# One fp32 attention and MLP kernel on one core: a new order of all its steps, without the warm-up steps behind the first, and with three instead of one joined product in seven sweeps

## The chip, the core and the metric

The kernel runs on one core of one Trainium2 chip. The time is that of one execution on the device, in microseconds (us); the timed runs of a kernel are told by their median. Of the engines TensorE (PE) does matmuls into PSUM (eight banks of 512 fp32 columns), VectorE (DVE) and ScalarE (ACT) read PSUM and SBUF, and SyncE (SP) issues nearly all transfers, in one queue and in order. GpSimd has almost nothing to do.

## What is computed

```python
def attention(x, state):            # x: 8 x 8 x 512 x 64, state: 8 x 8 x 32 x 64
    a = softmax(x @ state.T / 8)    # every row of x reads the 32 rows of state
    xread = a @ state
    a2 = softmax(state @ x.T / 8)   # every row of state reads the 512 rows of x
    sread = a2 @ x
    return concatenate([xread, sread], axis=2)     # 544 rows of 64 per head

x = attention(...).transpose(0, 2, 1, 3).reshape(4352, 512)
h = x @ w_in                        # 512 x 2048
g = log(1 + exp(h))                 # softplus
out = g @ w_out                     # 2048 x 512
```

All in fp32, with outputs of 8 x 544 = 4352 rows of 512.

## The kernel before

An fp32 number is held as a high and a low part, and one fp32 product is three matmuls in a faster format: high by high, high by low, low by high. A split into the two parts is one ACT copy (names that end in `h`: `gh`, `vh`, `wh`) and one DVE subtraction behind it (`gl`, `vl`, `wl`; line 328).

The weights come as 64-bit words and are turned into fp32 by three steps each: `ch` on ACT, `cu` and `cr` on DVE. The letter behind a step's name in the table of steps chooses the form: `ch` is an activation Prelu (letter A, which needs its own table load on ACT) or a Copy (C, which needs none); `cu` is one int32 operation (V) or two uint16 operations (W).

For each of the 8 batches b: the scores (`B.Qb`, from `Lz.b` and `Lt.b.i`, loads of state and x), a softmax over state in steps `qk`, `A`, `M`, `Ms`, `m` (Exp), `N`, `Nm`, `D`, `ah`, `al`; the first product of the MLP with state folded into w_in (`B.Vb.c`), `h.b.f` (six matmuls of 512 columns into one bank, 16 values of f), softplus `s`. The softmax the other way is `E` (row maximum), `e` (Exp), `r`, `H` (a transpose on DVE, stored by `Se` and loaded again by four `Le.b.j`), then the read group `B.Rb` (64 matmuls), `X.b` (a scaling), `T.b`, `th`, `tl`. The rows of state of all batches are a ninth batch, `h.8`, at the end.

The second product of batch 0 is done directly (steps `m.0.f.c`, accumulated in four banks). That of the other batches is done in 15 sweeps (b, s), each over half of a batch's rows, by a scheme with 7 products for 8 (Strassen's, in Winograd's form). A sweep has 8 blocks u; a block needs the stored softplus values (`Tr`, a load from `td`), three DVE additions `sfa`, `sfb`, `sfc` (lines 744 to 747), a split `gh`, `gl` of 128x896, and then on PE the steps `p.b.s.u.j`: X and Y with two products each, Z with two, Q with one. The sums of products stay in banks over the 8 blocks and are then added together by `e1` to `e6` (`e1` on ACT, the others on DVE at line 773; Z by one 128x512 operation `e5`).

A product with 256 columns is three matmuls of 256 columns (line 766). Product 6 (Q) is *wide* in all sweeps but the last: high by high and high by low are one matmul of 512 columns (line 762), low by high one of 256 (line 763) into the same bank, whose two halves are added when it is emptied. So a wide product takes a whole bank:

```python
if pi in wide:
    nc.tensor.matmul(at(bank), g(0), r(wform(u, m)(slice(0, 2))), start=first, ...)
    nc.tensor.matmul(at(bank)[:, 0:256], g(1), r(wform(u, m)(0)), start=False, ...)
    continue
```

The order of everything is a table, `PLAN`, written out by hand: 2833 entries `step:engine:places`, where T is PE, A and C are ACT, V and W are DVE, S is the SP queue, and the places are PSUM banks (0 to 7) and slots of one SBUF arena. Each engine does its steps in the order of the table and waits where data or a place isn't ready. Steps `w.i` (line 615) are warm-up steps: two transposes of the identity into a bank that nobody reads. The table names 14 of them; ten matmuls at the program's start (line 888) are apart from these.

Of the kernel before, what the change touches and what calls it, by code (L numbers as in the profile page):

```python
# [960 lines left out]
```

## Time and profile before

| | before |
|---|---|
| time, three runs | 630.94 us median (630.7 to 631.95) |
| profiled execution | 633.1 us, of which the span of instructions is 631.3 |
| PE busy | 617.0 us, 98% |
| DVE busy | 504.0 us, 80% |
| ACT busy | 397.2 us, 63% |
| granted TensorE clock | 1.00 throughout |
| HBM | 222 GB/s |

The span runs from the first to the last instruction of the profiled execution. PE's matmuls overlap at their ends, so that a busy share near 100% says that it rarely waited and not that each matmul is as short as it could be. Table loads aren't counted as busy time of ACT.

### The profile page before, as it was taken

The numbers are of one execution on the slowest core, as the hardware profiler recorded it, in microseconds if no ns is written. First come the engines' busy times: TensorE is split into PE (matmuls) and PEld (weight loads), VectorE is DVE, ScalarE is ACT, GpSimd is POOL, SyncE is SP. The second block draws the span as 40 slices with busy tenths as digits, with TensorE's granted clock in tenths as the row PEclk, the third lists the DMA queues.
The fourth block names the chain that finished last, engine by engine and source line by source line (L and its number), as shares of the span: only waits on it lengthen the run. The fifth ranks groups of instructions, "written<-read, shape, count | busy, mean of one in ns | idle before, by whom it ended". The sixth has DMA issues, their size and how long they took to land.

```text
span 631.3 us, 12414 instructions
## 1 busy us (share of the span) xinstructions
PE 617.0 (98%) x4604; PEld 530.2 (84%) x4604; DVE 504.0 (80%) x1081; ACT 397.2 (63%) x659; POOL 1.0 (0%) x7
## 2 busy tenths in 40 slices
...
GB/s 343 415 226 327 289 232 240 255 231 399 353 19 216 193 200 254 294 206 281 241 294 319 255 189 257 266 224 124 288 128 271 208 246 141 138 107 33 152 51 35
DMA packets 64253, 141.07 MB, mean 223 GB/s; under 512 B 7360, under 2 KB 17600, under 8 KB 64192
## 3 DMA queue, kind: packets, MB, share of 16 engines
...
HBM read 83.10 MB, written 57.15 MB: 222 GB/s over the span
## 4 chain that ended last, share of the span: by engine, by line
PE 70%; DVE 14%; DMA 10%; issue 2%; ACT 2%; SPq 2%; DVEq 0%; ACTq 0%
PE h L331 21%; PE pk_X L766 9%; PE pk_Y L766 9%; PE pk_Z L766 9%; PE acc L331 7%; DVE arena L328 4%; DMA arena<-td 3%; PE pk_Q L762 3%; PE h L820 2%; PE vp L331 2%; DMA arena<-vd 2%; PE vq L331 2%; SPq L319 1%; DVE arena L744 1%; PE pk_Q L763 1%
## 5 line engine op out<-in xcount | busy, mean ns | idle before, releaser
L312 ACT CAST arena<-arena 128x512 fp32r<-128x512 f32 (+2 forms) x255 | 185.8, 763 | 140.2 <-DVE arena L747 46.5
L328 DVE TENSOR_TENSOR arena<-arena,arena 128x512 fp32r<-128x512 f32 (+2 forms) x255 | 213.5, 858 | 58.3 <-ACT arena L312 56.1
L331 PE MATMUL h<-arena,arena 128*128 128x512 f32 x760 | 190.3, 399 | 0.0
L331 PEld LDWEIGHTS h<-arena,arena 128*128 128x128 f32 x760 | 138.3, 188 | 40.0 <-issue 4.2
L766 PE MATMUL pk_Y<-arena,arena 128*128 128x256 f32 x720 | 106.2, 284 | 0.4 <-DVE arena L328 0.4
L766 PE MATMUL pk_X<-arena,arena 128*128 128x256 f32 x720 | 105.5, 283 | 0.0
L766 PE MATMUL pk_Z<-arena,arena 128*128 128x256 f32 x696 | 103.8, 284 | 0.4 <-DVE arena L328 0.4
L766 PEld LDWEIGHTS pk_X<-arena,arena 128*128 128x128 f32 x720 | 96.6, 189 | 5.9
L766 PEld LDWEIGHTS pk_Y<-arena,arena 128*128 128x128 f32 x720 | 94.9, 190 | 1.1 <-DVE arena L328 0.6
L766 PEld LDWEIGHTS pk_Z<-arena,arena 128*128 128x128 f32 x696 | 92.2, 191 | 1.8 <-issue 0.8
L719 ACT ACTIVATE arena<-h 128x512 f32<-128x512 f32 x112 | 66.6, 613 | 29.8 <-PE h L331 25.7
L744 DVE TENSOR_TENSOR arena<-arena 128x256 f32<-128x256 f32 x120 | 49.5, 419 | 25.0 <-DMA arena<-td 23.9
L331 PE MATMUL acc<-arena,arena 128*128 128x512 f32 x192 | 45.7, 396 | 0.0
L762 PE MATMUL pk_Q<-arena,arena 128*128 128x512 f32 x112 | 44.8, 401 | 0.0
L331 PEld LDWEIGHTS acc<-arena,arena 128*128 128x128 f32 x192 | 35.8, 188 | 8.1 <-issue 1.0
L747 DVE TENSOR_TENSOR arena<-arena 128x128 f32<-128x128 f32 x120 | 33.6, 287 | 1.7
L746 DVE TENSOR_TENSOR arena<-arena 128x128 f32<-128x128 f32 x120 | 33.4, 287 | 1.4
L763 PE MATMUL pk_Q<-arena,arena 128*128 128x256 f32 x112 | 31.4, 280 | 0.0
L820 PE MATMUL h<-sreadT,arena 128*128 128x512 f32 x64 | 22.8, 393 | 0.0
L762 PEld LDWEIGHTS pk_Q<-arena,arena 128*128 128x128 f32 x112 | 21.3, 190 | 1.3 <-issue 0.8
L378 DVE SCALAR_TENSOR_TENSOR arena<-arena,arena 128x512 int32<-128x512 int32 x31 | 21.0, 688 | 0.5
L763 PEld LDWEIGHTS pk_Q<-arena,arena 128*128 128x128 f32 x112 | 21.3, 190 | 0.0
...
## 6 DMA issues: line engine op xcount, KB each, us to landing
...
arena<-td SPq DMA_DIRECT2D x112, 256.0 KB, 4.4
...
```

The source lines that it names most:

```text
L312: nc.scalar.copy(dst, src)
L328: lambda e: eng(e).tensor_tensor(r(dlo()), src(), dhi(), ALU.subtract))
L331: nc.tensor.matmul(dst, lhs, rhs, start=start, stop=stop)
L378: nc.vector.scalar_tensor_tensor(u, h2().bitcast(I32), 3, u, ALU.logical_shift_left, ALU.bitwise_or)
L719: nc.scalar.activation(t[:, :, 0::3] if i == 0 else t[:, :, 1:3], src.rearrange("p (s c t) -> p s c t", s=2, t=P), AF.Softplus)
L744: op(f"sfa.{k}", "V", t, [f"t.{k}:a"], lambda e, g=blocks: nc.vector.tensor_tensor(g()[:, 0:2], g()[:, 4:7:2], g()[:, 7:8].broadcast_to([P ...
L746: op(f"sfb.{k}", "V", [t[0], f"t.{k}:a"], [f"t.{k}:b"], lambda e, g=blocks: nc.vector.tensor_tensor(g()[:, 2], g()[:, 1], g()[:, 4], ALU.add))
L747: op(f"sfc.{k}", "V", [t[1], f"t.{k}:b"], [f"t.{k}:c"], lambda e, g=blocks: nc.vector.tensor_tensor(g()[:, 3], g()[:, 5], g()[:, 2], ALU.s ...
L762: nc.tensor.matmul(at(bank), g(0), r(wform(u, m)(slice(0, 2))), start=first, stop=False, skip_group_check=True)
L763: nc.tensor.matmul(at(bank)[:, 0:256], g(1), r(wform(u, m)(0)), start=False, stop=True, skip_group_check=True)
L766: nc.tensor.matmul(at(bank)[:, 256 * half:256 * half + 256], g(gi), r(wform(u, m)(wi)), start=first and pi == ps[0] and i == 0, stop=i == ...
L820: nc.tensor.matmul(hb, r(w[:, 0, cs]), r(at("sreadT")[:, :, kt, :]), start=kt == 0, stop=False, skip_group_check=True)
```

## The change

`PLAN` is a new table with 2897 entries. `WIDE` names seven sweeps in which products 4, 5 and 6 are wide: Z's two products then take a bank each (Z and W) and a step each, so that a block has five steps of PE (`p.b.s.u.2` is Z, `.3` W, `.4` Q) and a sweep five banks, and `e5` becomes four additions of 128x256 (`e5`, `e5l`, `e7`, `e7l`). The code for that was there and not in use. Of the warm-up steps only `w.0` stays. The forms of some steps change: `cu.2.0` to `cu.2.3` from W to V and `ch.2.0` to `ch.2.3` from C to A, `cu.o3` from V to W and `ch.o3` from A to C, with three such pairs later; `X.1` and `X.7` go from ACT to DVE. Of the table the diff shows the line with most of the warm-up steps, and the line of the new table with the step that follows them.

```diff
-WIDE = {}
+WIDE = {(4, 1): (4, 5, 6), (5, 0): (4, 5, 6), (5, 1): (4, 5, 6), (6, 0): (4, 5, 6), (6, 1): (4, 5, 6), (7, 0): (4, 5, 6), (8, 0): (4, 5, 6)}
...
-ah.1.0:A:42 Wl.0:V: ah.0.0:A:32 w.4:T:2 w.5:T:2 w.6:T:2 w.7:T:2 w.8:T:2 w.9:T:2 w.10:T:2 w.11:T:2 m.0.3.3:T: Wl.1:V: ah.0.1:A:34 al.1.0:V: D.1.1:T:2 Lo.4:S:38
...
+Li.2.0:S:22 D.1.0:T:1 wl.3:V: m.0.2.2:T: ah.1.0:A:24 N.1.1:V: m.0.3.3:T: Lo.4:S:26 Nm.1.1:V: cu.1.0:V:28 D.1.1:T:4 cu.1.1:V: m.0.3.1:T: al.1.0:V: ah.1.1:A:42
...
-            used = [f"acc.{b}.{x}.{c}:{f1}" for b, x, f0, fe in RUNS if f0 <= f1 < fe for c in range(4)]
+            used = [f"W.{f1}:u{b}{c}" for b in PLAIN for c in range(4)]
...
-            op(f"m.{k}.{c}", "T", [f"g.{k}:h", f"g.{k}:l", f"W.{f}:h", f"W.{f}:l"] + ([f"{acc}:{f - 1}"] if f > f0 else []), [f"{acc}:{f}"], gemm2)
+            op(f"m.{k}.{c}", "T", [f"g.{k}:h", f"g.{k}:l", f"W.{f}:h", f"W.{f}:l"] + ([f"{acc}:{f - 1}"] if f > f0 else []), [f"{acc}:{f}", f"W.{f}:u{b}{c}"], gemm2)
```

The last two edits name differently what `Wh` waits for, with the same effect. All lines behind the table are five further down in the changed kernel.

Three places of the new order follow, each before and after. First DVE near the end of the ramp, before: from the last softmax product of batch 1 (`Nm.1.1`, L464) to the low part `al.1.0` of its transposed softmax (the last row). Between them are `cfa`, `cfb` (L595, L597: combinations of w_out) and five splits (L328), the third of them `gl.0.3`.

```order
L464 TENSOR_TENSOR arena_432<-arena_432,sm 128x512
L595 SCALAR_TENSOR_TENSOR arena_185<-arena_314,arena_317 128x256
L595 SCALAR_TENSOR_TENSOR arena_185<-arena_416,arena_314 128x256
L597 TENSOR_TENSOR arena_317<-arena_317 128x256
L597 TENSOR_TENSOR arena_314<-arena_314 128x256
L328 TENSOR_TENSOR arena_414<-vp_0_1_366,arena_414 128x512
L328 TENSOR_TENSOR arena_499<-arena_416,arena_499 128x512
L328 TENSOR_TENSOR arena_502<-arena_183,arena_502 128x512
L328 TENSOR_TENSOR arena_384<-arena_317,arena_384 128x256
L328 TENSOR_TENSOR arena_425<-arena_314,arena_425 128x256
L328 TENSOR_TENSOR arena_508<-ab_0_486,arena_508 128x512
```

The same place on DVE in the changed kernel: from the splits `gl.0.3` and `wl.3` (the first two rows) over the second softmax sum and product (L463 to L469) to `al.1.0`.

```order
L333 TENSOR_TENSOR arena_454<-arena_425,arena_454 128x512
L333 TENSOR_TENSOR arena_459<-arena_403,arena_459 128x512
L463 TENSOR_REDUCE sm<-arena_403 128x16
L464 TENSOR_SCALAR sm<-sm 128x16
L465 RECIPROCAL sm<-sm 128x16
L469 TENSOR_TENSOR arena_403<-arena_403,sm 128x512
L375 TENSOR_SCALAR arena_190<-arena_246 128x512
L375 TENSOR_SCALAR arena_190<-arena_257 128x512
L333 TENSOR_TENSOR arena_487<-ab_0_478,arena_487 128x512
```

The combinations and the two half splits of 128x256 are gone from here; the splits stand ahead of the softmax product, and behind it come only two `cu.1.q` (L375).

Second the SP queue around the loads for `B.Q6`, before: `in_zp_dram` is `Lz.6` (state), `in_xt_dram` are `Lt.6.0` and `Lt.6.1` (x), `td` and `te` are spilled values.

```order
L319 DMA arena_2338<-in_xt_dram 128x1024
L322 DMA out_dram<-arena_185 128x512
L319 DMA arena_2510<-td_110 128x512
L319 DMA arena_767<-td_111 128x512
L319 DMA arena_185<-in_xt_dram 128x1024
L322 DMA td_126<-arena_2988 128x1024
L319 DMA arena_3438<-td_113 128x512
L319 DMA arena_2673<-in_zp_dram 128x256
```

And in the changed kernel, from `Lz.6` to `Lt.6.1`:

```order
L324 DMA arena_403<-in_zp_dram 128x256
L327 DMA out_dram<-arena_2216 128x512
L324 DMA arena_2885<-td_112 128x512
L324 DMA arena_2086<-td_110 128x512
L327 DMA te_71<-arena_337 128x512
L327 DMA te_71<-arena_3216 128x512
L324 DMA arena_403<-qd_81 128x512
L324 DMA arena_2216<-td_111 128x512
L324 DMA arena_3410<-in_xt_dram 128x1024
L327 DMA td_126<-arena_2897 128x1024
L324 DMA arena_337<-in_xt_dram 128x1024
```

The state load stood behind both x loads and now stands ahead of both.

Third DVE in sweep (3,0), before: the rows up to the split `gl.3.0.7` (the last row) and behind `gl.3.0.5`; L438 is the transpose `A.6.g` of the scores of batch 6.

```order
L746 TENSOR_TENSOR arena_3438<-arena_3438 128x128
L747 TENSOR_TENSOR arena_3438<-arena_3438 128x128
L744 TENSOR_TENSOR arena_949<-arena_949 128x256
L746 TENSOR_TENSOR arena_949<-arena_949 128x128
L438 STREAM_TRANSPOSE arena_2673<-sc_1_3678 128x512
L438 STREAM_TRANSPOSE arena_2347<-sc_0_3677 128x512
L747 TENSOR_TENSOR arena_949<-arena_949 128x128
L328 TENSOR_TENSOR arena_2044<-arena_3438,arena_2044 128x896
```

And in the changed kernel, the last twelve rows up to `gl.3.0.7`; ahead of them, behind `gl.3.0.5`, stand one more `sfa` (L749) and the two `A.6.g` (L443). L485 and L486 are `E.3.0`, L445 `M.6.g`, L459 `Ms.6.0`, L528 `H.3.0`.

```order
L751 TENSOR_TENSOR arena_2885<-arena_2885 128x128
L485 TENSOR_REDUCE nm<-arena_3202 128x1
L486 TENSOR_SCALAR nm<-nm 128x1
L752 TENSOR_TENSOR arena_2885<-arena_2885 128x128
L749 TENSOR_TENSOR arena_3685<-arena_3685 128x256
L445 TENSOR_REDUCE mx<-arena_2216 128x16
L751 TENSOR_TENSOR arena_3685<-arena_3685 128x128
L445 TENSOR_REDUCE mx<-arena_403 128x16
L752 TENSOR_TENSOR arena_3685<-arena_3685 128x128
L459 TENSOR_TENSOR arena_403<-arena_403,mx 128x512
L528 STREAM_TRANSPOSE arena_2216<-arena_3202 128x4x4x32
L333 TENSOR_TENSOR arena_2169<-arena_2885,arena_2169 128x896
```

Row maximum, maxima, difference and transpose have moved ahead of the split, and with them the additions of the next sweep's first block.

## Rows read from the trace of the kernel before

**Rows 1.** The page: busy time, share of span and instructions of each engine.

```profile
PE 617.0 (98%) x4604; PEld 530.2 (84%) x4604; DVE 504.0 (80%) x1081; ACT 397.2 (63%) x659; POOL 1.0 (0%) x7
```

**Rows 2.** Stretches: from:to, length, busy PE, PEld, DVE, ACT, POOL; clock, DMA share, GB/s.

```profile
44.00:60.00 16.00, 15.94 (x119) 10.33 (x118) 15.38 (x33) 15.53 (x29) 0.00 (x0) 1.00 0.82 309
100.00:160.00 60.00, 60.00 (x371) 42.21 (x370) 46.54 (x90) 58.42 (x109) 0.00 (x0) 1.00 0.76 287
250.00:270.00 20.00, 18.25 (x234) 16.46 (x233) 17.73 (x43) 12.47 (x20) 0.00 (x0) 1.00 0.93 289
290.00:310.00 20.00, 18.99 (x181) 17.08 (x181) 12.66 (x34) 11.98 (x20) 0.00 (x0) 1.00 0.75 238
330.00:350.00 20.00, 17.94 (x185) 15.34 (x184) 18.21 (x41) 14.14 (x22) 0.00 (x0) 1.00 0.93 318
350.00:370.00 20.00, 19.36 (x184) 16.98 (x183) 18.89 (x48) 14.77 (x27) 0.00 (x0) 1.00 0.78 235
550.00:600.00 50.00, 50.00 (x376) 47.93 (x375) 41.77 (x95) 25.53 (x49) 0.00 (x0) 1.00 0.31 101
```

**Rows 3.** Timeline of the ramp, all engines: start, length (us), engine, line, operation.

```profile
30.02 1.28 ACT L363 ACT_TABLE_LOAD   x1
35.25 1.28 ACT L646 ACT_TABLE_LOAD   x1
37.21 3.85 PE L615 MATMUL wp<-ident 128*128 128x128 f32 x16
38.16 1.96 DVE L328 TENSOR_TENSOR arena<-arena,arena 128x512 fp32r<-128x512 f32 x4
40.82 0.94 PE L331 MATMUL acc<-arena,arena 128*128 128x512 f32 x3
44.12 4.25 PE L331 MATMUL h<-arena,arena 128*128 128x512 f32 x18
```

**Rows 4.** DVE by line and shape: count, then busy us, mean ns, idle time.

```profile
L328 DVE TENSOR_TENSOR arena<-arena,arena 128x896 fp32r<-128x896 f32 x120 | 129.6, 1087 | 39.4 <-ACT arena L312 37.4 <-PE tp L539 1.1 <-PE pk_Q L762 0.5
L328 DVE TENSOR_TENSOR arena<-arena,arena 128x512 fp32r<-128x512 f32 x119 | 79.2, 686 | 19.0 <-ACT arena L312 18.6
L744 DVE TENSOR_TENSOR arena<-arena 128x256 f32<-128x256 f32 x120 | 49.5, 419 | 25.0 <-DMA arena<-td 23.9 <-DMA arena<-vd 0.5
L747 DVE TENSOR_TENSOR arena<-arena 128x128 f32<-128x128 f32 x120 | 33.6, 287 | 1.7
L373 DVE TENSOR_SCALAR arena<-arena 128x512 uint16<-128x512 uint16 x19 | 8.8, 462 | 0.0
L370 DVE TENSOR_SCALAR arena<-arena 128x512 int32<-128x512 int32 x13 | 5.3, 416 | 0.0
L773 DVE TENSOR_TENSOR arena<-pk_Z,arena 128x512 f32<-128x512 f32 x14 | 9.6, 682 | 0.0
L773 DVE TENSOR_TENSOR arena<-pk_Q,arena 128x256 f32<-128x256 f32 x29 | 12.1, 417 | 0.0
```

**Rows 5.** Timeline of PE at the read group `B.R4`.

```profile
250.99 0.88 PE L766 MATMUL pk_Y<-arena,arena 128*128 128x256 f32 x6
253.41 1.10 PE L331 MATMUL rp<-arena,arena 128*32 128x64 f32 x64 [1.54 <-DMA td<-arena]
```

**Rows 6.** Timeline of PE at the score group `B.Q6`.

```profile
328.71 1.56 PE L331 MATMUL h<-arena,arena 128*128 128x512 f32 x6
332.33 1.09 PE L331 MATMUL sc<-arena,arena 64*32 64x512 f32 x16 [2.06 <-DMA arena<-in_zp_dram]
```

**Rows 7.** Timeline of PE: X steps one block apart, sweeps (7,0) and (7,1).

```profile
558.13 0.87 PE L766 MATMUL pk_X<-arena,arena 128*128 128x256 f32 x6
560.63 0.88 PE L766 MATMUL pk_X<-arena,arena 128*128 128x256 f32 x6
606.65 0.88 PE L766 MATMUL pk_X<-arena,arena 128*128 128x256 f32 x6
609.17 0.88 PE L766 MATMUL pk_X<-arena,arena 128*128 128x256 f32 x6
```

More of the change, by code (lines that the diff above doesn't have):

```diff
@@ L93 @@
-B.K3.1:T:5,4 s.3.4.0:A: gl.0.7:V: ch.o10:C:64 Sv.3.2.1:S: h.2.12:T:7 cv.3.1.0:A:11 cu.o10:W:52 Td.3.4:S: cv.3.1.1:A:53 ch.o8:C:78 cr.o10:V: Sv.3.1.0:S:
-h.2.13:T:1 s.3.5.1:A: D.4.0:V:79 ch.o9:C:64 cu.o8:W:3 h.2.14:T:6 Lo.11:S:34 gh.0.8:A:88 cu.o9:W:71 gh.0.10:A:40 Lo.13:S:80 s.2.6.0:A:54 cr.o8:V: h.2.15:T:3
-Sv.3.1.1:S: wh.10:A:86 gl.0.8:V: wh.8:A:38 cr.o9:V: h.3.12:T:2 s.2.6.1:A: gl.0.10:V: Td.3.5:S: wh.9:A:16 wl.10:V: s.2.7.0:A:32 h.3.13:T:5 Td.2.6:S: wl.8:V:
-ch.o7:C:59 wl.9:V: s.2.7.1:A: cu.o7:W:78 Lo.12:S:44 h.3.14:T:4 s.3.6.0:A:96 s.3.6.1:A: cfa.4:V:64 Lv.4.0.0:S:94 cr.o7:V: m.4.1:A: h.3.15:T:0 cfb.4:V:
@@ new lines @@
+Li.3.2:S:56 vh.1.1.0:A:38 Li.3.3:S:46 vh.1.1.1:A:66 vl.1.1.0:V: Lo.5:S:76 vh.0.1.0:A:82 Lo.6:S:88 vl.1.1.1:V: h.1.3:T:0 vh.0.1.1:A:48 vl.0.1.0:V: ch.2.0:A:62
+vl.0.1.1:V: ch.2.1:A:65 h.1.5:T:6 E.0.1:V: ch.2.2:A:52 ch.2.3:A:53 cu.2.0:V:96 h.1.4:T:5 cu.2.1:V: uh.0.2:A:54 cr.2.0:V: s.1.0.0:A:58 cr.2.1:V: h.1.6:T:1
+cu.2.2:V:92 Sf.2.0:S: cu.2.3:V: cr.2.2:V: s.1.2.1:A:80 h.1.7:T:4 cr.2.3:V: s.1.2.0:A: ul.0.2:V: Sf.2.1:S: s.1.3.0:A:86 cfa.0:V:62 Lt.2.0:S:22 kh:A:18
+B.V0.2+V1.2:T:2,6,5,1 cfb.0:V: Lt.2.1:S:70 s.1.3.1:A: kl:V: Lt.3.0:S:72 ch.3.0:C:65 cfc.0:V: Lt.3.1:S:52 ch.3.1:C:94 cfd.0:V: Td.1.2:S: cu.3.0:W:38 ch.3.2:C:66
@@ new lines @@
+Sv.0.1.1:S: D.2.0:V:70 s.0.12:A:71 h.0.14:T:1 Td.1.7:S: D.2.1:V:72 ah.2.0:A:24 M.3.1:V: ah.2.1:A:42 h.0.15:T:3 Lt.4.0:S:62 al.2.0:V: s.0.13:A:73 Lt.4.1:S:80
+s.0.14:A:8 al.2.1:V: uh.2.1:A:58 Ms.3.0:V: B.K0.0:T:5,7 s.0.15:A:70 ul.2.1:V: m.3.0:A: B.V2.0+V3.0:T:4,6,2,0 Ms.3.1:V: cfa.1:V:72 cfb.1:V: cfc.1:V:
+cv.0.0.0:A:56 B.K0.3:T:1,3 Lz.4:S:57 N.3.0:V: vh.2.0.1:A:22 Sv.0.0.0:S: vh.2.0.0:A:44 vl.2.0.1:V: vh.3.0.0:A:20 vl.2.0.0:V: vh.3.0.1:A:30 B.K0.2:T:5,6
+cv.0.0.1:A:36 vl.3.0.0:V: h.2.0:T:4 cv.0.3.0:A:37 Sv.0.0.1:S: vl.3.0.1:V: cv.0.3.1:A:56 Sv.0.3.0:S: Nm.3.0:V: m.3.1:A: Sv.0.3.1:S: h.2.1:T:7 cfd.1:V:
```

427 lines of the change are left out of this document (214 added, 213 removed).

## Prediction

> **What bounds the kernel now.** I read the page first, then the busy time by stretch, then the timelines where TensorE (PE) is idle. PE works 617.0 of 631.3 us, VectorE (DVE) 504.0, ScalarE (ACT) 397.2 [rows 1], so PE bounds the whole and the span can fall in three ways only: fewer steps on PE, shorter ones, or less waiting in front of them. The stretches differ. From 44 to 60 us DVE is busy 15.38 and ACT 15.53 of 16 us [rows 2]: there PE takes what these two deliver, and the eight warm-up steps in a row at 37.21 (3.85 us, sixteen transposes) stand where PE would otherwise idle [rows 3]. From 100 to 160 us ACT is busy 58.42 of 60 and PE never stops [rows 2]. In four 20 us stretches between 250 and 370 us PE is idle 1.75, 1.01, 2.06 and 0.64 us [rows 2]: mostly loads that come late. From 550 to 600 us PE has no idle time at all [rows 2].
>
> The profiled execution took 633.1 us, 2.2 more than the median of the three timed ones (630.94). The changes below are summed against 633.1 and then set off from the median. Times of PE steps are differences of starts, since one matmul's end overlaps the next one's start.
>
> **The ramp: warm-ups out, work reordered.** Thirteen warm-up steps of two transposes go; their starts are about 0.48 us apart (3.85 us for eight), 6.3 us in all. That is not the gain, since DVE and ACT would be waited for instead. The ramp ends with `B.V0.3+V1.3`, the last group of batches 0 and 1. What stands ahead of it on DVE: out go `cfa.1` and `cfb.1` (0.42 each, priced as other 128x256 adds), `Wl.0` and `Wl.1` (the same size, 0.42 each) and `ul.0.1` (0.69); in come `Tl.0` (0.69) and `cfd.0` (0.42). Net 2.37 - 1.11 = 1.26 us less. The four `cu.2.q` turn from two uint16 operations (0.462 each; the second of the pair is of the same form and size) into one int32 operation (0.416): 0.51 less each, 2.03 in all. `cu.o3` turns the other way, 0.51 more. Net: 2.8 us less DVE work ahead of that group [rows 4]. On ACT the Exp `e.0.1`, which needs a table load before it and one behind it, now comes after the group: at 1.28 a load [rows 3] that is 2.6 us less ahead of it, beside the step itself. So DVE allows 2.8 and ACT about as much, of a possible 6.3 on PE. The first places agree. The step behind the eight warm-ups, `m.0.3.3` at 40.82, needed `gl.0.3`, the second of four operations at 38.16 (done about 39.5), and that needed `s.0.3`, which stood on ACT behind a table load at 30.02, `ch.o3`, two Exp, four `ch.1.q` and a table load at 35.25 [rows 3]. Now `ch.o3` is a Copy and `s.0.3` comes right behind it, ahead of all of these: some 5 us sooner, so that `m.0.3.3` can follow `D.1.0` at once, near 37. The next steps wait for `al.1.0` and `al.1.1`. Nine operations of 0.42 to 0.69 us stood between the last softmax product and `al.1.0`; two `cu` and the split itself stand there now (first two order excerpts). I therefore let the first `h.1.0` move from 44.12 to about 41.5. DVE and ACT stay full up to 60 us, so nothing more is gained there; from 60 to 100 us they have room. From 100 to 160 us ACT is full, with the same steps and table loads in it, so it starts sooner and ends sooner; a few tenths go where ACT's copies and softplus steps stand in a new order. **Ramp: -2.7 us**, bounds -4.2 (DVE's idle time is used as well) and -1.0 (the first steps' input loads hold it).
>
> **The middle, 230 to 430 us.** Here PE waited for loads. `B.R4` came 253.41 - 250.99 - 0.72 = 1.70 us later than the Y step before it lets it [rows 5], `B.Q6` 332.33 - 328.71 - 1.40 = 2.22 us late (1.40 is an `h` step of six matmuls at 0.23) [rows 6], `B.R1` at 291 about 1.0 (the idle time of 290 to 310) and `B.R0` at 266 some 0.2 (1.75 idle between 250 and 270, less the 1.54 of `B.R4`). Sum 5.1. Some ten further steps, each less than 0.8 us behind what steps of its kind take, come to 2.8 together (the 0.64 us between 350 and 370 are of these); 7.9 in all.
>
> What the new order does to each: `B.Q6` waited for the state load `Lz.6`, which was issued behind two `xt` loads and four `td` transfers. Now that load stands ahead of these (third and fourth excerpts), and 14 us of PE steps lie between it and the group instead of 5: the 2.22 go. `B.R4` stands one product step (0.72) later: 1.70 - 0.72 = 1.0 remains. `B.R0` and `B.R1` come 0.35 and 1.7 us of PE steps later relative to their loads: both waits go. Against this `B.R5` has 4.9 us between the last load and itself where it had 6.4, and `B.R6` 6.7 where it had 11.8. The groups that waited, above, got their data only after 6 to 7 us; so `B.R5` may wait between 0 and 2.2, for which I take 0.6. Loads after: 1.6 of the 5.1.
>
> The price is on DVE. Between `gl.3.0.5` and `gl.3.0.7`, the splits that two blocks of products wait for, stand thirteen other operations and the split itself (last two excerpts): two stacked transposes, two maxima, a difference, the row maximum and a transpose of 128x512 (seven, priced like the split of this size at 0.69; the row maximum's small scaling is left out), two triples of 0.42 + 0.29 + 0.29 and the split at 1.09 [rows 4], 8.0 us by durations and some 7 by starts (the four operations at 38.16, 2.2 us by durations, took 1.96 [rows 3]). PE has two blocks of 2.50 us to do meanwhile [rows 7]. So `p.3.0.7.1` waits about 2.0 us. Before, two of these seven stood there and the other five behind `gl.3.0.7`, where they cost PE some 1.4 of the 2.8 us in small pieces up to 365 us. A second place, the splits of sweep (2,0), and `X.5`, a scaling that the next `h` step waits for, cost perhaps 0.5 each. Small waits of 1.3 us I leave as they are. So 2.8 becomes 2.0 + 1.0 + 1.3 = 4.3. **Middle: (1.6 + 4.3) - 7.9 = -2.0 us**, bounds -4.5 (DVE's new place is covered) and +1.5 (`B.R5` waits 2.2 and the DVE places add 1.5).
>
> **The wide products.** A block of seven products with Q alone wide takes 560.63 - 558.13 = 2.50 us; in the last sweep, where Q is narrow, 609.17 - 606.65 = 2.52 [rows 7]. One wide product thus saves about 0.016 us by the blocks; by the steps themselves (0.36 for three matmuls of 256 columns, 0.35 for one of 512 and one of 256) 0.009. Seven sweeps x 8 blocks x 2 products = 112: 1.0 to 1.8 us, and I take 1.2. On DVE one 128x512 eviction (0.682) becomes four of 128x256 (0.417): 0.99 us more in each of seven sweeps [rows 4]. From 550 to 600 us DVE is busy 41.77 of 50 [rows 2], so this has cover; banks are tighter (five of eight in a sweep), for which I add 0.2. **Wide: -1.0 us**, bounds -1.8 and +0.5.
>
> On this term the Trainium skill bears (page "TensorE: Matmul & The Clock Gate", section "Back-to-back issue gap"): it gives the warm spacing of single matmuls as N/2.4 ns plus about 2.5, so that joining two of 256 columns saves one 2.5 ns. By that 112 joins would give an estimate of 0.3 us; the blocks in the trace show three to six times as much.
>
> **Sum.** -2.7 - 2.0 - 1.0 = -5.7: 627.4 on the profiled execution's time, **625.2 us** against the median. A difference under 0.2% (1.26 us) is about what a measurement of this kernel can't tell from no change.
>
> **Rivals.**
> *Waits change places.* DVE is the second engine everywhere, and the new order puts more in front of it. If `B.R5` waits in full, the DVE places cost 1.5 more than I say and ACT between 100 and 160 us gives back 1.5 of the ramp, the middle ends near +1 and the ramp at -1.2: 630.94 - 1.2 + 1 - 1 = 629.7, faster or the same. For it: 15.38 of 16 and 58.42 of 60 us busy [rows 2]. Against it: the largest single wait of before (2.2) is plainly gone. 0.18.
> *All stalls go.* The ramp gives 4.2, the middle 4.5, the wide products 1.6: 620.6. Against it: DVE's 7 to 8 us in front of a 5 us stretch. 0.10.
> *Slower: the bank squeeze.* A wide sweep holds five banks, and at its end W is free only after the evictions of X, Y and twice 0.42, each of which can stand behind a split of 1.09 [rows 4]; the next sweep's fifth bank, or an `h` group, then waits. It decides when each of the seven sweep ends costs PE more than (5.7 + 1.3) / 7 = 1.0 us; at 2 us each the time is 639. For it: DVE at 84% from 550. Against it: sweeps with four banks show no wait there at all. 0.06.
> *Slower: the clock.* The warm-ups kept PE active where it would idle. The granted clock was 1.00 (2.4 GHz) in every stretch of [rows 2], also around idle times of 1.54 and 2.06 us [rows 5, 6]. If PE now fell to 1.2 GHz from 44 to 60 us, its 15.94 us of work there would take twice as long: 630.94 - 5.7 + 15.9 = 641. The new idle pieces in the ramp are under 2 us each by my walk, so 0.02.
> The same page of the Trainium skill, in its table under "Why this matters for your kernels", warns that a PE left idle between bursts goes back to the lower clock. No run here shows that so far.
>
> **Numbers.** Forecast 0.64 (622 to 628), waits change places 0.18 (half faster, half the same), all stalls go 0.10, slower 0.08. Faster 0.83, same 0.09, slower 0.08. The range, 620.5 to 630.0, leaves out the slower cases, half of the one in which all stalls go, and the upper edge of the one in which waits change places; the forecast's own is 622 to 628.
>
> **What would show it.** Ramp: first `h.1.0` at 41 to 42, no wait over 1 us before 60; DVE or ACT still over 15 of 16 us there. Middle: no idle time at `B.Q6` and `B.R1`, about 1 at `B.R4`, some 2 us of PE waits for DVE's split in the last blocks of sweep (3,0). Wide: blocks of 2.47 to 2.49 us and no idle time on PE from 430 on. It is wrong if `h.1.0` stays near 44, if the read groups 5 or 6 wait over 2 us, or if PE waits at the ends of wide sweeps.

## The result and the profile after

The changed kernel takes 624.4 us (median of four runs, 623.81 to 624.99) against 630.82 for the kernel before in the same comparison (628.75 to 631.95): a ratio of 0.9903, 95% interval 0.9884 to 0.9922. Run once more beside other kernels it took 624.76 against 631.62, ratio 0.9894 [0.9864, 0.9925]. Forecast were 625.2 us, 620.5 to 630.0, and faster with 0.83. Its profiled execution took 624.3 us, with a span of 622.5.

The page of the changed kernel, busy time by engine and the granted clock of PE in forty slices:

```profile
PE 610.8 (98%) x4466; PEld 521.6 (84%) x4466; DVE 508.5 (82%) x1104; ACT 395.9 (64%) x655; POOL 1.0 (0%) x7
...
PEclk9999999999999999999998999999999999999999
```

PE has 6.2 us less work than in [rows 1], with 138 matmuls fewer: 112 joined ones and 26 transposes of the thirteen warm-ups. DVE has 4.5 us more. One slice of the clock reads 8; there is none like it before.

Busy time of the changed kernel by stretch (from:to, length, busy PE, PEld, DVE, ACT, POOL; clock, DMA share, GB/s), some of them stretches of [rows 2], then the whole of the wide sweeps up to 600 us and some of 1 us:

```profile
20.00:28.00 8.00, 7.85 (x55) 4.42 (x40) 7.35 (x15) 7.99 (x15) 0.00 (x0) 1.00 1.03 407
36.00:44.00 8.00, 8.00 (x60) 5.29 (x59) 6.22 (x12) 5.72 (x12) 0.00 (x0) 1.00 0.88 317
44.00:60.00 16.00, 15.30 (x91) 11.02 (x90) 15.90 (x35) 15.96 (x31) 0.00 (x0) 1.00 0.98 338
250.00:270.00 20.00, 19.79 (x194) 18.26 (x193) 16.61 (x42) 14.66 (x23) 0.00 (x0) 1.00 0.86 267
290.00:310.00 20.00, 20.00 (x166) 18.39 (x168) 17.10 (x40) 11.54 (x19) 0.00 (x0) 1.00 0.88 274
330.00:350.00 20.00, 17.63 (x160) 15.26 (x159) 18.54 (x45) 11.14 (x18) 0.00 (x0) 0.91 0.65 211
...
430.00:600.00 170.00, 170.00 (x1184) 155.90 (x1183) 139.84 (x310) 81.32 (x131) 0.00 (x0) 1.00 0.49 161
...
333.00:334.00 1.00, 0.00 (x0) 0.00 (x0) 1.00 (x2) 0.69 (x2) 0.00 (x0) 1.00 0.50 205
334.00:335.00 1.00, 0.60 (x5) 0.60 (x6) 1.00 (x3) 0.62 (x1) 0.00 (x0) 1.00 0.60 200
335.00:336.00 1.00, 1.00 (x9) 1.00 (x8) 1.00 (x2) 0.29 (x2) 0.00 (x0) 0.72 0.90 262
336.00:337.00 1.00, 1.00 (x6) 0.90 (x5) 1.00 (x3) 0.33 (x1) 0.00 (x0) 0.50 0.87 277
```

From 44 to 60 us DVE and ACT are as good as full. PE's idle time in 250 to 270 and 290 to 310 is all but gone (0.21 us, 2.76 before). From 430 to 600 us PE doesn't stop once. One hole remains, at 330 to 350, and behind it PE runs for some 3.4 us at 1.2 GHz (clock 0.50).

The timeline of PE in the changed kernel (start, length, line, operation), at the first `h.1.0`, `B.R4`, `B.Q6`, the hole in sweep (3,0), and two X steps one block apart in a wide sweep:

```profile
38.13 1.07 PE L336 MATMUL h<-arena,arena 128*128 128x512 f32 x4
...
246.36 0.88 PE L771 MATMUL pk_Z<-arena,arena 128*128 128x256 f32 x6
247.17 1.10 PE L336 MATMUL rp<-arena,arena 128*32 128x64 f32 x64
...
324.96 1.09 PE L336 MATMUL sc<-arena,arena 64*32 64x512 f32 x16
...
331.75 0.50 PE L771 MATMUL pk_Y<-arena,arena 128*128 128x256 f32 x2
334.40 0.74 PE L771 MATMUL pk_Y<-arena,arena 128*128 128x256 f32 x4 [2.14 <-DVE arena L333]
334.97 1.10 PE L771 MATMUL pk_Z<-arena,arena 128*128 128x256 f32 x6
335.87 0.63 PE L767 MATMUL pk_Q<-arena,arena 128*128 128x512 f32 x1
...
336.51 1.48 PE L771 MATMUL pk_X<-arena,arena 128*128 128x256 f32 x6
337.79 0.63 PE L767 MATMUL pk_Q<-arena,arena 128*128 128x512 f32 x1
...
338.43 3.13 PE L336 MATMUL h<-arena,arena 128*128 128x512 f32 x12
...
555.95 0.87 PE L771 MATMUL pk_X<-arena,arena 128*128 128x256 f32 x6
...
558.43 0.88 PE L771 MATMUL pk_X<-arena,arena 128*128 128x256 f32 x6
```

`B.Q6`, which waited 2.06 us in [rows 6], has no wait; `B.R4` comes 247.17 - 246.36 - 0.72 = 0.1 us late instead of 1.7 [rows 5]. Step `p.3.0.7.1` (331.75) stops in its midst for DVE's split: it takes 334.97 - 331.75 = 3.22 us where 0.72 is usual, 2.50 too long. The clock falls at about 335.4, 1.0 us after PE has begun again. The five steps from `pk_Z` on are longer by it: `pk_Z` 0.90 instead of 0.72, the two `pk_Q` 0.64 instead of 0.35 each, `pk_X` 1.28 instead of 0.72, and `h.5.12` 1.59 instead of 1.40 (`h.5.13` starts at 340.02). That is 0.18 + 0.29 + 0.56 + 0.29 + 0.19 = 1.5 us. A block of the wide sweep takes 558.43 - 555.95 = 2.48 us, 2.50 before [rows 7].

**Where the time went.** The starts of the same PE step in two executions, subtracted, give the gain up to there. Against the profiled execution of before, in us:

| step (start before) | after | after, once more |
|---|---|---|
| `D.0.0`, first step of the ramp's bulk (15.68) | -1.68 | -1.28 |
| `h.1.0` (44.12) | -6.00 | -5.62 |
| `B.V0.3+V1.3`, end of the ramp (66.85) | -5.76 | -5.34 |
| `p.1.0.0.0`, first product (192.31) | -5.34 | -4.97 |
| `h.5.13` (347.39) | -7.37 | -7.14 |
| `p.5.0.0.0`, end of the middle (440.36) | -8.02 | -8.44 |
| `p.7.1.7.3`, in the last block of products (626.09) | -8.78 | -9.20 |

The first line is no effect of the change. PE's first score group, the same sixteen matmuls, took 1.96 us in that execution of before and 1.09 after:

```profile
6.49 1.96 PE L331 MATMUL sc<-arena,arena 64*32 64x512 f32 x16 [0.81 <-DMA arena<-in_zp_dram]
...
6.18 1.09 PE L336 MATMUL sc<-arena,arena 64*32 64x512 f32 x16 [1.07 <-DMA arena<-in_zp_dram]
```

The trace's clock records show why. They begin, with 1.00, at 10.50 us in before and at 4.35 us in the changed kernel; there are none ahead of that, so the "1.00 throughout" of the table of before holds from 10.50 us on only. The length of the group says which level PE had until then: in experiment 1 such a group takes 1.85 us while the granted clock falls to 0.50. Over all profiles a late begin goes with a late start: the records begin at 10.50, 9.85 and 7.08 us where `D.0.0` starts at 15.68, 15.32 and 14.39, and at 4.04 to 6.50 where it starts at 13.90 to 14.15, one of these with before's own ramp (`before_state_sooner`, below). So some 1.7 of the 8.8 us is a late start of that one execution. Without it the ramp gave 5.34 - 1.7 = **3.6** (3.3 in the second execution), the middle **2.7** (3.5), and the stretch from 440 on **0.8** (0.8). Measured from `before_state_sooner`, whose ramp is before's, the ramp's gain is the same: `p.1.0.0.0` starts there at 190.60 us, 3.6 us later than in the changed kernel.

### The profile page after: what moved, and what is told of

Same layout as the page of the kernel before. It is cut to its first block, busy times and chain, and to the rows that moved or that the text cites. A ratio compares the mean times of both kernels' runs of the same rounds, so it can differ in the third digit from the quotient of the medians.

```text
span 622.5 us, 12168 instructions
## 1 busy us (share of the span) xinstructions
PE 610.8 (98%) x4466; PEld 521.6 (84%) x4466; DVE 508.5 (82%) x1104; ACT 395.9 (64%) x655; POOL 1.0 (0%) x7
## 4 chain that ended last, share of the span: by engine, by line
PE 86%; DMA 6%; DVE 6%; issue 1%; ACT 1%; SPq 0%; DVEq 0%; ACTq 0%
PE h L336 25%; PE pk_X L771 13%; PE pk_Y L771 13%; PE pk_Z L771 6%; PE acc L336 6%; PE pk_Q L767 4%; PE h L825 2%; PE pk_W L767 2%; PE pk_Z L767 2%; DMA arena<-in_xn_dram 2%; PE pk_Q L768 2%; PE vp L336 2%; DVE arena L333 2%; PE vq L336 2%; PE rp L336 1%; PE h L826 1%
## 5 line engine op out<-in xcount | busy, mean ns | idle before, releaser
L333 DVE TENSOR_TENSOR arena<-arena,arena 128x896 fp32r<-128x896 f32 (+2 forms) x255 | 212.7, 856 | 53.8 <-ACT arena L317 52.6
L724 ACT ACTIVATE arena<-h 128x512 f32<-128x512 f32 x112 | 66.2, 612 | 39.0 <-PE h L336 32.3
L749 DVE TENSOR_TENSOR arena<-arena 128x256 f32<-128x256 f32 x120 | 49.4, 417 | 10.0 <-DMA arena<-td 9.7
L771 PE MATMUL pk_Z<-arena,arena 128*128 128x256 f32 x360 | 54.0, 285 | 0.0
L771 PEld LDWEIGHTS pk_Z<-arena,arena 128*128 128x128 f32 x360 | 47.9, 191 | 1.1 <-issue 0.8
L767 PEld LDWEIGHTS pk_Q<-arena,arena 128*128 128x128 f32 x112 | 21.5, 192 | 3.9 <-issue 0.8
L767 PE MATMUL pk_W<-arena,arena 128*128 128x512 f32 x56 | 22.7, 405 | 0.0
L767 PE MATMUL pk_Z<-arena,arena 128*128 128x512 f32 x56 | 22.2, 397 | 0.0
```

Source lines behind the costliest of these rows:

```text
L333: lambda e: eng(e).tensor_tensor(r(dlo()), src(), dhi(), ALU.subtract))
L724: nc.scalar.activation(t[:, :, 0::3] if i == 0 else t[:, :, 1:3], src.rearrange("p (s c t) -> p s c t", s=2, t=P), AF.Softplus)
L749: op(f"sfa.{k}", "V", t, [f"t.{k}:a"], lambda e, g=blocks: nc.vector.tensor_tensor(g()[:, 0:2], g()[:, 4:7:2], g()[:, 7:8].broadcast_to([P ...
L771: nc.tensor.matmul(at(bank)[:, 256 * half:256 * half + 256], g(gi), r(wform(u, m)(wi)), start=first and pi == ps[0] and i == 0, stop=i == ...
```

## The experiments

The theory that was put to the test first is the prediction's own: the new order on DVE and ACT is what lets the warm-ups go. Its rival: the warm-ups alone held up PE, and with it DVE and ACT. For the middle: DVE is short of time, so that moving its work moves the wait, against a wait that a better place removes. Ratios are to the kernel before, timed beside each on the same chip. Of the table `PLAN` the diffs show the entries that an edit touches.

**1. Before without the warm-ups** (`before_no_warmups`): is their removal the ramp's gain, or the new order on DVE and ACT?

```diff
-w.1:T:3 ... w.2:T:2 w.3:T:2 ... w.4:T:2 w.5:T:2 w.6:T:2 w.7:T:2 w.8:T:2 w.9:T:2 w.10:T:2 w.11:T:2 ... w.12:T:4 w.13:T:4
```

> The kernel before without its warm-up steps w.1 to w.13, nothing else changed. Theory A (in the ramp PE waits for DVE and ACT, and the warm-ups mostly stand in those waits): m.0.3.3 starts when gl.0.3 is done, near 39.5 us instead of 40.8, and about 1 us of that is left at 67 us, so that the whole is 0.7 to 1.8 us faster, 629 to 630. Theory B (the warm-ups themselves were on the path): 13 x 0.48 = 6.3 us faster, near 624.5. Theory C (they keep the clock up): granted clock under 1.00 somewhere between 36 and 60 us and no gain, 631 to 636.

Measured: 631.76 us (627.04 to 633.53), ratio 0.9989 [0.9964, 1.0015]. In the ramp `p.1.0.0.0` starts 4.92 us sooner, 3.2 without the start: nine tenths of what the whole change gave there, with DVE's and ACT's work untouched. Stretches of this kernel (columns as above):

```profile
20.00:28.00 8.00, 8.00 (x57) 4.60 (x57) 7.10 (x14) 7.97 (x14) 0.00 (x0) 1.00 1.03 413
...
36.00:44.00 8.00, 7.89 (x49) 5.91 (x56) 7.96 (x18) 8.00 (x17) 0.00 (x0) 1.00 0.71 253
...
327.00:328.00 1.00, 1.00 (x14) 0.15 (x1) 0.36 (x1) 0.04 (x1) 0.00 (x0) 0.50 1.07 264
```

And the same stretches of the kernel before:

```profile
20.00:28.00 8.00, 7.94 (x53) 3.49 (x52) 5.79 (x12) 6.85 (x13) 0.00 (x0) 1.00 1.02 411
...
36.00:44.00 8.00, 7.59 (x40) 5.15 (x39) 7.28 (x17) 6.64 (x14) 0.00 (x0) 1.00 0.45 172
```

And of `before_state_sooner`, with before's ramp and an ordinary start:

```profile
20.00:28.00 8.00, 7.94 (x55) 4.02 (x54) 5.79 (x12) 6.85 (x13) 0.00 (x0) 1.00 1.02 411
...
36.00:44.00 8.00, 7.65 (x37) 5.37 (x38) 7.29 (x16) 6.66 (x14) 0.00 (x0) 1.00 0.49 182
```

Before, DVE and ACT had idle time ahead of 44 us (0.7 to 2.2 of 8 us), because PE's transposes delayed the results that feed them; without the warm-ups they are nearly full (7.10 to 8.00). The late start has no part in this, since `before_state_sooner` shows the same idle time. In the changed kernel, where their work stands in another order, DVE and ACT are busy 6.22 and 5.72 us from 36 to 44, and there PE is busy for all of the 8 us.

But most of the gain doesn't reach the end: 3.2 us would be a ratio of 0.9949, and the interval begins at 0.9964. PE's timeline of this kernel at `B.Q6`:

```profile
321.75 1.09 PE L330 MATMUL h<-arena,arena 128*128 128x512 f32 x4
326.08 1.85 PE L330 MATMUL sc<-arena,arena 64*32 64x512 f32 x16 [3.24 <-DMA arena<-in_zp_dram]
```

The idle time is 3.24 where it was 2.06 [rows 6], and the clock falls as the group begins (0.50 from 327 to 328): `sc` takes 1.85 instead of 1.09. Against before this kernel is 7.41 us ahead at `B.R1`, 6.25 at `B.Q6`, 4.68 at `h.5.12` behind the fallen clock, and 3.77 at `p.5.0.0.0`. So the state load does come sooner, but by less than PE does; the DMA engines are busy 0.90 of the time from 310 to 330. The profiled execution took 629.31 us, the third shortest of twelve, and so shows only a part of what the median loses.

**2. The same with part of the new order on ACT and DVE** (`before_no_warmups_act_order`): `ch.o3` a Copy, `s.0.3` right behind it, and the splits of `g.3` and `W.3` ahead of the table load.

```diff
-ch.o3:A:92
+ch.o3:C:92 s.0.3:A:22
-cu.o3:V:86
+cu.o3:W:86
-wh.3:A:26 vl.1.0.1:V: gh.0.3:A:28 wl.3:V: ... gl.0.3:V: ah.1.0:A:42
+gh.0.3:A:28 wh.3:A:26 ... gl.0.3:V: wl.3:V: vl.1.0.1:V: ... ah.1.0:A:42
```

> As the kernel without warm-ups, and in the ramp ch.o3 as a Copy (cu.o3 then as two operations), s.0.3 right behind it, gh.0.3 and wh.3 ahead of the four ch.1.q, and on DVE gl.0.3, wl.3 and vl.1.0.1 ahead of cfa and cfb. Theory A: this order is what lets the warm-ups go; gl.0.3 is done 2.5 to 4 us sooner, and at 67 us PE is 2 to 3 us ahead of the kernel before, so 628 to 629. Theory B: no more than the kernel without warm-ups gains, the two within 0.5 us of each other.

Measured: 633.44 us (629.01 to 635.87), 1.0023 [1.0001, 1.0046]: no better than without this edit, by the medians worse. The ramp's gain falls from 3.2 to 1.3. PE's timeline:

```profile
34.85 0.63 PE L424 MATMUL ab<-ident,arena 128*128 128x128 f32 x4 [1.75 <-DVE arena L463]
...
48.88 4.76 PE L330 MATMUL h<-arena,arena 128*128 128x512 f32 x18 [1.40 <-ACT arena L311]
```

What the prediction gave as the reason, `s.0.3` sooner by these moves, makes other work late on the same two engines: the softmax product (L463) that `D.1.0` waits for, and the cast that `h.1.5` needs.

**3. After with the warm-ups** (`after_with_warmups`): the thirteen steps put back at the same PE steps, in free banks.

```diff
-N.1.1:V: m.0.3.3:T:
+N.1.1:V: w.4:T:2 w.5:T:2 w.6:T:2 w.7:T:2 w.8:T:2 w.9:T:2 w.10:T:2 w.11:T:2 m.0.3.3:T:
```

(and `w.1`, `w.2` and `w.3`, `w.12` and `w.13` in the same way at `D.0.1`, `V.0.0.1.1` and `h.1.5`)

> The changed kernel with the 13 warm-up steps put back ahead of the same PE steps (D.0.1, V.0.0.1.1, m.0.3.3, h.1.5). Theory A: m.0.3.3 no longer has anything to wait for there, so the eight steps ahead of it cost what they take, and DVE and ACT, which are full up to 60 us, can only make part of it good: 2.5 to 4.5 us slower than the changed kernel, 627 to 629. Theory B: all 6.3 us come back, near 630.7. If the warm-ups still stood in waits, less than 1 us: under 625.4.

Measured: 627.58 us (625.8 to 628.67), 0.9931 [0.9913, 0.9948], some 3 us over the changed kernel by the medians, 2 by the ratios. Up to `p.1.0.0.0` it gains 1.02, less than the 1.5 of its start: the new order alone costs the ramp 0.5. PE's timeline and a stretch of it:

```profile
35.26 3.85 PE L621 MATMUL wp<-ident 128*128 128x128 f32 x16
...
42.18 2.21 PE L337 MATMUL h<-arena,arena 128*128 128x512 f32 x9
```

```profile
36.00:44.00 8.00, 7.65 (x39) 5.43 (x37) 5.44 (x11) 3.71 (x8) 0.00 (x0) 1.00 0.41 166
```

The sixteen transposes run while DVE and ACT idle (5.44 and 3.71 of 8): PE does useless work, and the others have nothing to do until it is over. With 1 this settles the ramp. Removal gives 3.2 in the old order and 3.6 + 0.5 = 4.1 in the new one; the order gives 0.4 on top at most.

**4. After without wide products** (`after_not_wide`): the Z steps whole again, one `e5`.

```diff
-WIDE = {(4, 1): (4, 5, 6), (5, 0): (4, 5, 6), (5, 1): (4, 5, 6), (6, 0): (4, 5, 6), (6, 1): (4, 5, 6), (7, 0): (4, 5, 6), (8, 0): (4, 5, 6)}
+WIDE = {}
...
-p.4.1.0.2:T:0 e5.4.0:V: p.4.1.0.3:T:7
+p.4.1.0.2:T:0 e5.4.0:V:
```

> The changed kernel with WIDE empty: in the seven sweeps the two Z products share a bank and a step of six matmuls of 256 columns again, with one eviction e5 of 128x512 at the place of e5; the order of all other steps stays. If one wide product saves 0.009 to 0.016 us as the blocks of before show, the kernel is 0.9 to 1.7 us slower than the changed one, near 625.5, and a block of these sweeps takes 2.50 instead of about 2.49 us. If only the spacing of two joined matmuls counted, 0.3 us slower. If the added evictions or the fifth bank cost more than they bring, it is faster than 624.4.

Measured: 627.79 us (625.25 to 629.84), 0.9934 [0.9911, 0.9957]. The medians differ by 3, and that is too much for the wide products: up to sweep (4,1) the two kernels are the same instructions, and this execution had lost 3.9 us there by late loads and a clock that fell behind a wait of 2.32 us at `p.3.0.7.1`. The mean granted clock of five of its six timed runs is 0.996 or 0.997, that of three of the ten of the changed kernel (with experiment 5). From `p.5.0.0.0` to the end it loses 0.17 on before, the changed kernel gains 0.76: six wide sweeps give 0.93 us, 96 joined products 9.7 ns each, 1.09 for all 112. In both PE is busy for the whole of the stretch from 430 to 600 us.

**5. The changed kernel once more** (`after_again`), beside 6 and 7: how much differs with nothing changed?

> The changed kernel once more, unchanged, so that the kernels beside it stand against it on the same chip, and for a second profile of it. If the middle stretch varies by chance from execution to execution, its waits at B.R0, B.R2 and p.3.0.7.1 differ from those of the first profile by a microsecond or more while the ramp and the time from 430 us on agree within 0.2 us. Time 623.5 to 627.

Measured: 624.76 us (622.39 to 627.0), 0.9894 [0.9864, 0.9925]. Ramp and end agree within 0.4 and 0.1 us with the first execution; the middle differs by 0.8. The wait at `p.3.0.7.1` is there again, and the clock stays. Its PE timeline and a stretch behind the wait:

```profile
336.15 0.74 PE L771 MATMUL pk_Y<-arena,arena 128*128 128x256 f32 x4 [2.13 <-DVE arena L333]
```

```profile
337.00:338.00 1.00, 1.00 (x10) 0.96 (x9) 1.00 (x3) 0.54 (x1) 0.00 (x0) 1.00 0.89 254
```

`B.R0` waited 1.33 us here and 0.37 in the first execution.

**6. After with four warm-ups ahead of the wait** (`after_kept_busy`): does the fallen clock matter?

```diff
-vh.5.3.0:A:28 p.3.0.7.1:T:
+vh.5.3.0:A:28 w.23:T:2 w.22:T:2 w.21:T:2 w.20:T:2 p.3.0.7.1:T:
```

> The changed kernel with four warm-up steps (eight transposes into a free bank) ahead of p.3.0.7.1, where PE waited 2.14 us for gl.3.0.7 and the granted clock then fell to 0.50 for some 3.5 us. Theory: the wait itself stays, but PE isn't idle in it and the clock stays at 1.00, so the steps up to h.5.13 take 1.5 to 2 us less and the kernel is up to 1.9 us faster than the changed one where its clock falls. Rival: the clock has nothing to do with the wait; the same time or up to 1 us slower, where the transposes reach beyond the wait.

Measured: 625.12 us (623.16 to 630.29), 0.9909 [0.9879, 0.9938], the same as the changed kernel. PE's timeline:

```profile
334.26 1.87 PE L620 MATMUL wp<-ident 128*128 128x128 f32 x8
335.89 1.20 PE L771 MATMUL pk_Y<-arena,arena 128*128 128x256 f32 x6
```

The warm-ups took 335.89 - 334.26 = 1.63 us of the wait, and `p.3.0.7.1` was 0.31 us too long behind them: 1.94 in all. The clock stayed at 1.00 here, but it does so without the edit too, so that one profile tells nothing. Two of the eight timed runs have a mean clock of 0.997, and they are the longest (628.33 and 630.29). What the fall costs at this place stays untested.

**7. The late split first** (`after_split_first`): `gl.3.0.7` ahead of `E.3.0`, the maxima and the difference of batch 6 behind `gl.3.1.0`.

```diff
-A.6.1:V:18 p.3.0.5.2:T: sfb.3.0.7:V: E.3.0:V:
+A.6.1:V:18 gl.3.0.7:V: p.3.0.5.2:T: E.3.0:V:
...
+gl.3.1.0:V: M.6.0:V: Ms.6.0:V: m.6.0:A: M.6.1:V: Le.5.1:S:
```

> The changed kernel with another order on DVE and ACT in front of p.3.0.7.1: the additions and the split of its block (sfb, sfc, gh, gl.3.0.7) come ahead of the row maximum, and M.6.0, Ms.6.0 and M.6.1 behind gl.3.1.0. Theory (that place was short of DVE's order, and what DVE has to do can be put off): the wait at p.3.0.7.1 goes, the clock stays at 1.00, and some 1 us comes back at p.3.1.0.3 to h.5.14: 2 to 3.5 us faster than the changed kernel. Rival (DVE is short of time there in all): the whole wait turns up at p.3.1.0.3, h.5.12 or h.6.0, and the time is within 0.7 us.

Measured: 624.26 us (622.94 to 626.58), 0.9893 [0.9867, 0.992]: no gain. PE's timeline:

```profile
337.39 2.70 PE L336 MATMUL h<-arena,arena 128*128 128x512 f32 x10 [1.66 <-DVE arena L333]
```

The wait has gone from `p.3.0.7.1` and stands in `h.5.12`, which starts at 335.10 and is followed by `h.5.13` at 338.54: 3.44 instead of 1.40. `h.5.13` so starts 1.5 and 1.7 us sooner than in the two executions of the changed kernel, but at `p.4.1.0.0` only 0.6 and 0.2 us are left. DVE is busy 19.56 of the 20 us from 330 to 350, so whatever goes first, something is late.

**8. More of DVE's work put off** (`after_dve_put_off`): on top of 7 the next block's splits first, the softmax of batch 6 later, and `B.R0` two product steps later.

```diff
-gl.3.1.0:V: M.6.0:V: Ms.6.0:V: m.6.0:A: M.6.1:V:
+gl.3.1.0:V: vl.5.3.0:V: M.6.0:V: vh.5.3.1:A:48 vl.5.3.1:V: sfa.3.1.1:V: sfb.3.1.1:V: sfc.3.1.1:V: gh.3.1.1:A:4 Ms.6.0:V: gl.3.1.1:V: M.6.1:V: Ms.6.1:V:
...
-e4.3.0:V:
+e4.3.0:V: N.6.0:V: Nm.6.0:V: N.6.1:V: Nm.6.1:V:
```

> The changed kernel with the order of after_split_first carried on: behind gl.3.1.0 DVE does what the next PE steps need (vl.5.3.0, vl.5.3.1, the additions and split of block 1 of sweep (3,1)) and puts the softmax of batch 6 off (M, Ms, N and Nm in between and behind e4.3.0), X.5 comes ahead of m.6.0 on ACT, and B.R0 two product steps later. Theory (DVE isn't short of time over 20 us, only its order was wrong): the wait of 2 us, at p.3.0.7.1 in the changed kernel and at h.5.13 in after_split_first, shrinks to under 1 us in all, B.R0 waits no more (0.4 to 1.3 us), and the kernel is 1.5 to 3.5 us faster than the changed one, 621 to 623. Rival (DVE is short over the whole stretch up to 350 us): the wait turns up at h.5.14, p.3.1.0.2 or h.6.0, and only B.R0's share is left: 0.3 to 1.3 us faster.

Measured: 625.72 us (624.77 to 626.91), 0.9909 [0.9888, 0.993]: not faster. PE's waits in this kernel (who waited for what: us in total, times, longest):

```profile
PE tp L544 <- ACT arena L724: 1.0, 1, 1.0
PE rp L336 <- DMA arena<-in_xn_dram: 0.8, 1, 0.8
PE pk_X L771 <- DVE arena L333: 0.7, 1, 0.7
PE pk_Y L771 <- DVE arena L333: 0.7, 1, 0.7
```

The wait of 2.1 us is gone, and `h.5.13` starts at 338.07, about 2 us sooner than in the changed kernel. But `T.5` now waits 1.0 us for a softplus on ACT (L724), `B.R3` 0.8 for a load, and `p.3.1.4.0` and `p.2.0.7.1` (the latter behind the moved `B.R0`) 0.7 each for a split. At `p.4.1.0.0` this execution is 1.2 and 1.7 us behind the two of the changed kernel: what was gained is lost again, and more.

**9 and 10. The state load sooner in the old order**, without the warm-ups (`before_no_warmups_state_sooner`) and with them (`before_state_sooner`): is `Lz.6` what eats the ramp's gain in 1?

```diff
-B.R2:T:2 sfa.3.0.4:V:
+B.R2:T:2 Lz.6:S:59 sfa.3.0.4:V:
...
-H.5.0:V:58 Lz.6:S:59
+H.5.0:V:58
```

> The kernel before without warm-ups, and with the state load Lz.6 issued right behind B.R2, ahead of the transfers td and Tr.3.0.7 (its slot is not free sooner). Theory (the ramp's gain is given back where a load of the middle arrives late and the clock then falls): Lz.6 lands about 1 us sooner, the wait at B.Q6 goes from 3.4 to some 2.4 us, and where that keeps the clock at 1.00 the kernel is 1 to 2.7 us faster than without warm-ups alone, 629 to 630.5. Rival (the wait at B.Q6 is that of the x load or of the whole of the transfers): no difference beyond 0.5 us.

> The kernel before, with its warm-ups, and with the state load Lz.6 right behind B.R2, as in before_no_warmups_state_sooner. Theory (the wait at B.Q6 takes what the ramp gives): by itself it takes 1 to 2.2 us off the wait at B.Q6, so 629 to 630.5; the warm-ups' removal on top of it (0.9960 of the kernel before) is then worth what the load alone doesn't bring. If the load's place alone brought all of 0.9960, the warm-ups would be worth nothing; if it brings nothing, B.Q6 waits for something else as long as the warm-ups stand.

Measured: 629.41 us (625.67 to 632.42), 0.996 [0.9934, 0.9986] without the warm-ups; 631.08 (628.9 to 633.24), 0.9988 [0.9971, 1.0005] with them. In both profiles the wait of 2 to 3 us at `B.Q6` is gone. Without the warm-ups:

```profile
322.53 1.09 PE L330 MATMUL sc<-arena,arena 64*32 64x512 f32 x16
```

With them, PE's waits name DVE's splits instead:

```profile
PE pk_Z L766 <- DVE arena L328: 2.2, 1, 2.2
PE pk_X L766 <- DVE arena L328: 1.6, 1, 1.6
```

The twelve runs of experiment 9 lie in two groups, five from 625.67 to 626.86 us and six from 630.28 to 632.42, with one between; the profile is of the shortest. The clock has a part in it. One fall of 3.4 us makes a mean granted clock of 0.997 over a run, as in the profiled one of the changed kernel. At 0.997 or less are 32 of 59 runs of the kernel before timed beside these experiments, 11 of 12 in experiment 1, but 3 of 12 in experiment 9 and none of 12 in experiment 10. So the place of this one load changes how often the clock falls.

Neither edit alone shows a gain that can be told from no change (0.9989 and 0.9988), and both together do (0.996). That they help each other the times alone don't show: 0.9989 x 0.9988 = 0.9977 lies in the interval of both together. That is still some 4 us short of the changed kernel (0.4% against 1.0%); the wide products are 1.1 of these and the ramp's order 0.4.

## Why the prediction was right, and where it was not

**The sum** was right: 625.2 forecast, 624.4 and 624.76 measured. Of its three terms the wide products came out as costed and the middle near it; the ramp's was too small, and it came near by another mechanism than the one given, so that this part is luck.

**The ramp: mis-sized, and the reason given for it was wrong.** Forecast -2.7, measured -3.6. The step that failed: "That is not the gain, since DVE and ACT would be waited for instead." Removal alone gives 3.2 to 4.1 of these 6.3 us (experiments 1 and 3), more than the whole term; only the rest is waited for. The prediction read [rows 2] at 44 to 60, where DVE and ACT are full, and counted on them as if they were full ahead of it too; in 20 to 28 and 36 to 44 they had room (5.79 to 7.28 of 8), and it was the warm-ups that made it, by holding up what PE hands them. Its walk along single steps (`m.0.3.3` near 37, `h.1.0` near 41.5) took the warm-ups to fill time in which PE would wait anyway; `h.1.0` started at 38.13 instead (39.8 with the late start added). The reason put in its place, 2.8 us less DVE work and an earlier `s.0.3`, is worth 0.4 at most, and a part of it alone was a loss (experiment 2). "DVE and ACT stay full up to 60 us, so nothing more is gained there" held: 15.90 and 15.96 of 16. The upper case, "DVE's idle time is used as well" at -4.2, was nearer to what happened. Between the ramp's end and `p.1.0.0.0` 0.4 us of the gain is lost, the "few tenths" that the prediction gave to ACT there.

**The middle: right in kind.** Forecast -2.0; 2.7 and 3.5 in two executions, 0.1 of it wide products. The medians give another estimate: 6.4 in all, less 3.6 and 1.1, is 1.7. Piece by piece: the waits for loads went from 5.1 to 0.5 us in the first execution and 1.4 in the second, forecast 1.6. `B.Q6` and `B.R1` have none, as said; `B.R4` 0.1 where 1.0 was forecast; `B.R5` none where 0.6 was put; `B.R0` still has 0.37 and 1.33, and was to have none. The price on DVE was found where it was put: "`p.3.0.7.1` waits about 2.0 us"; it was 2.50, in both. The timeline of the transfer (SP) and of DVE in the changed kernel shows why it is more:

```profile
319.53 0.32 SPq L324 DMA_DIRECT2D arena<-td  x1
...
327.42 0.43 DVE L749 TENSOR_TENSOR arena<-arena 128x256 f32<-128x256 f32 x1 [2.21 <-DMA arena<-td]
...
332.67 0.70 DVE L528 STREAM_TRANSPOSE arena<-arena 128x512 f32<-128x512 f32 x1
333.30 1.05 DVE L333 TENSOR_TENSOR arena<-arena,arena 128x896 fp32r<-128x896 f32 x1
```

DVE stood idle for 2.21 us in front of `sfa.3.0.7`, for a transfer issued at 319.53, and only then began the chain to `gl.3.0.7` (333.30). From there to the split's end it takes 6.9 us, near the "7 by starts" that the prediction counted: the order on DVE was priced rightly, the load ahead of it was not looked at. In the second execution DVE stood idle 1.65 us at the same place; in experiment 6, where it didn't, the wait came to 1.94.

**What the prediction didn't see: what the ramp gives can be lost in the middle.** It added the two terms. In the old order most of the ramp's gain is lost again: the ratio is 0.9989 where 3.2 us would make 0.9949 (experiment 1), and the profile shows the largest piece at `B.Q6`, by the wait and the clock behind it. With the load of that group sooner, the clock falls in fewer runs and a gain is left (experiment 9). The new order has its loads ahead of where a PE that is some 5 us sooner needs them, which is the likely reason why the sum held; the prediction moved them for the waits of before alone, so that this too is luck.

**The wide products: right.** -1.0 forecast, 1.09 measured, with what the evictions and banks cost in it; no wait for a bank is seen. The blocks are 2.48 us, and PE has no idle time from 430 to 600. Of the two prices of a join, the one by the steps (0.009 us) is near the 0.0097 measured; the one by the blocks (0.016) was too high, and [rows 7] give 2.52 - 2.50 = 0.02 for it. The Trainium skill's page "TensorE: Matmul & The Clock Gate", section "Back-to-back issue gap", gives about 2.5 ns per single matmul beside its columns; for 112 joins that is an estimate of 0.3 us. By the runs a join is worth 9.7 ns.

**The rivals.** "Waits change places" happened in small: moving DVE's work (experiments 7 and 8) or a load (10) moved the wait each time. "All stalls go" (620.6) and "the bank squeeze" (639) did not happen. "The clock" was given 0.02 for the ramp, and there it stayed at 1.00; it fell in one of the two profiled executions at `p.3.0.7.1`, for a loss of 1.5 us, a place that the prediction had named for the wait and not for the clock. The Trainium skill's page "TensorE: Matmul & The Clock Gate" warns, in its table under "Why this matters for your kernels", of a fall behind idle time between bursts. The trace now shows one, 1.0 us behind a wait of 2.14 us.

**Open.** The middle differs by up to 0.8 us between executions of the same kernel, and single runs by up to 4.6 (622.39 to 627.0), so that its pieces below 1 us are not proven. A part of this is the clock: the two longest of the six runs of experiment 5, 626.82 and 627.0, have a mean clock of 0.996, and the two shortest 0.999 and 1.00. Some 2.5 us lie between both edits of experiment 9 and the changed kernel after 1.1 for the wide products and 0.4 for the ramp; what is left for them is the rest of the middle's order (`B.R4`, `B.R1` and the loads around them), which no run changed alone.
